# Two gated layers on one core: decays laid out by chunk, whole-chunk GpSimd operations, and a new order of all queues

## The chip, the core and the metric

The kernel runs on one core of a Trainium2 chip. The metric is the device time of one execution in microseconds, taken over several runs. A core has five instruction queues that run side by side and meet through semaphores: PE (TensorE, matrix products and transposes), VectorE (DVE in the profile), ScalarE (ACT), GpSimd (POOL) and SyncE (SP, which here issues all large transfers).

## The reference

Inputs are `x`, `r_gate` and `i_gate`, each 4 x 6336 x 256 float32, a vector `a_param` of 256, and the weights `w_val` (256 x 256), `conv_w` (5 x 256) and `w_out` (256 x 256). The first layer is a recurrence in time, the second a gated unit whose gate is a causal convolution of five taps:

```
log_a = 8 * sigmoid(r_gate) * log(clip(sigmoid(a_param)))
a = exp(log_a)
u = sqrt(max(1 - a*a, 1e-6)) * sigmoid(i_gate) * x
h[t] = a[t]*h[t-1] + u[t]                 # y = all h, for each batch
gate = sigmoid(sum over k of conv_w[k] * y[t-4+k])
out  = (gate * (y @ w_val)) @ w_out
```

## The kernel before

The four sequences are laid end to end: 25344 time steps of 256 channels. They are cut into 51 windows, mostly of 512 steps, and these into 28 chunks: chunks 0 and 1 of 256 steps, 2 of 512, 3 to 25 of two windows (1024 steps, chunk 26 has 512, chunk 27 256). Channels come in two halves of 128, called h. A window is loaded with time on the partitions; the recurrence wants channels on the partitions, so PE transposes in between.

One long string, `ORDER`, sets everything: it is a list of steps such as `ta.6` (a step's name, its chunk or window, sometimes the half) with the PSUM banks behind an `@`. The steps are written out in this order, so it is the order of each engine's queue. The steps of one chunk or window, with the lines of the profile:

- SP: `lr`, `li`, `lx` load a window of r, i and x (L292) into rings of four windows; `st` stores a window of the output (L546).
- ScalarE: `ta` and `tb` take tanh of r and i (L310, L313); `ex` makes the decays a with one exponential per half, for one chunk or a group of two (L378); `rt` takes the square roots of 1 - a*a for a batch of chunks (L405), usually three; `tg` is the gate's tanh (L502); `ca` copies an output window out of PSUM (L535). Tanh and exponential need one table of functions, the square root another, so there is a table load (L562) ahead of each run of `rt` and one behind it. `sa` squares a half of a chunk (L394, twice in the program).
- GpSimd: `sq` squares the decays of one half of one chunk into `ering` (L386); `pp` adds one to the tanh of i of a window (L320); `up` multiplies that by x (L332). `s_wcast` casts the weights once (L275 to L278).
- PE: `tr` transposes tanh of r (L357); `nt` transposes the square roots (L420), `xt` the gated inputs back (L461); `cv` is the convolution (L495), `vl` and `ou` the two products (L510, L525); `xp` carries x of three early windows through PSUM (L337). `wm` issues five products of 512 columns on the identity whose result nobody reads (L364).
- VectorE: `xg` multiplies the input by the root (L450); `sc` is the recurrence as a scan, one per half (L483); `gv` multiplies gate and value (L515); `cd` copies an output window (L533), where `ca` does not; `uv` is `up` for the three early windows (L346).

So a chunk goes: `lr`, `ta`, `tr`, `ex`, `sq`, `rt`, `nt`, `xg`, `xt`, `sc`, and then per window `cv`, `tg`, `vl`, `gv`, `ou`, `cd` or `ca`, `st`. The decays stand in `aring`, one half behind the other: `aring[:, h, ...]` has 5120 columns for each half, and a chunk has the same place in both. The squares of a chunk stand in `ering` with both halves side by side, so that one square root covers several chunks:

```
at = H * e_at[c] + h * clen[c]
return ering[:, at:at + clen[c]], aring[:, h, a_at[c]:a_at[c] + clen[c]]
```

## Time and profile before

| | |
|---|---|
| runs | 289.22, 287.34, 287.65 us; median 287.65 |
| profiled execution | span 286.4 us from the first to the last instruction; the page gives no other time for it |
| busy | PE 251.8 us, VectorE 246.8, ScalarE 273.6, GpSimd 241.6 |
| granted TensorE clock | 0.999 |
| transfers | 104.76 MB, mean 366 GB/s |

In the profile's rows a line such as "L378 ACT ACTIVATE aring<-banks,khf" is one group of instructions: the line of the kernel, the engine, the operation, what it writes and reads. A row of a timeline begins with the start in microseconds from the first instruction and the time that the row's instructions take together, and ends with the idle time of the engine ahead of it and what ended that. In a row of waits stand the total in microseconds, the number of waits and the longest. In a row of stretches each engine has its busy time in that stretch.

### The profile page before, as it was taken

The numbers are of one execution on the slowest core, as the hardware profiler recorded it, in microseconds if no ns is written. First come the engines' busy times: TensorE is split into PE (matmuls) and PEld (weight loads), VectorE is DVE, ScalarE is ACT, GpSimd is POOL, SyncE is SP. The second block draws the span as 40 slices with busy tenths as digits, with TensorE's granted clock in tenths as the row PEclk, the third lists the DMA queues.
The fourth block names the chain that finished last, engine by engine and source line by source line (L and its number), as shares of the span: only waits on it lengthen the run. The fifth ranks groups of instructions, "written<-read, shape, count | busy, mean of one in ns | idle before, by whom it ended". The sixth has DMA issues, their size and how long they took to land.

```text
span 286.4 us, 6382 instructions
## 1 busy us (share of the span) xinstructions
PE 251.8 (88%) x2552; PEld 171.1 (60%) x2576; DVE 246.8 (86%) x214; ACT 273.6 (96%) x198; POOL 241.6 (84%) x161
## 2 busy tenths in 40 slices
PE   1387778899999999988988999989989899999993
PEld 1253447456656767455756676656646774767562
DVE  4002898969999899999999999999999999999991
ACT  5999999999999999999999999999999999898984
POOL 1659589899999999999999999999996999874600
PEclk9999999999999999999999999999999999999999
DMA  7999999999999999999999999999999999994536
GB/s 243 384 373 407 409 403 408 388 366 376 410 408 366 418 367 392 414 410 334 405 364 413 411 332 356 420 416 419 415 401 333 359 416 406 364 356 170 192 150 256
DMA packets 29996, 104.76 MB, mean 366 GB/s; under 512 B 3335, under 2 KB 3854, under 8 KB 29966
## 3 DMA queue, kind: packets, MB, share of 16 engines
q1 hardware_dynamic: 29952, 104.35, 94.5%
q8 instruction: 20, 0.33, 0.5%
q14 instruction: 10, 0.08, 0.1%
q10 hardware_dynamic: 14, 0.01, 0.0%
HBM read 78.39 MB, written 25.95 MB: 364 GB/s over the span
## 4 chain that ended last, share of the span: by engine, by line
ACT 33%; PE 29%; DVE 14%; issue 12%; DMA 8%; SPq 1%; ACTq 0%; DVEq 0%
ACT ering L405 8%; PE banks L495 8%; DVE yring L483 7%; PE banks L525 7%; DMA rring<-in_r_gate_dram 6%; ACT tgring L502 6%; ACT taring L310 5%; ACT tbring L313 5%; ACT aring L378 5%; PE banks L510 5%; PE banks L461 3%; DVE tgring L515 3%; PE banks L420 3%; ACT L562 3%; DVE oring L533 2%
## 5 line engine op out<-in xcount | busy, mean ns | idle before, releaser
L386 POOL TENSOR_TENSOR ering<-aring 128x1024 f32<-128x1024 f32 (+2 forms) x54 | 91.5, 1714 | 16.7 <-ACT aring L378 16.4
L332 POOL TENSOR_TENSOR uring<-tbring,xring 128x1024 bf16<-128x1024 bf16 (+1 forms) x48 | 101.1, 2119 | 3.6 <-DMA xring<-in_x_dram 3.1
L483 DVE TENSOR_TENSOR_SCAN yring<-aring,yring,banks 128x1024 bf16<-128x1024 f32 (+5 forms) x50 | 101.7, 2064 | 2.1 <-PE banks L461 1.9
L495 PE MATMUL banks<-yring,diag 64*64 64x512 bf16 (+7 forms) x1080 | 62.1, 361 | 2.3 <-ACT aring L378 1.6
L515 DVE SCALAR_TENSOR_TENSOR tgring<-tgring,banks 128x1024 bf16<-128x1024 bf16 (+1 forms) x51 | 59.1, 1178 | 4.0 <-PE banks L510 3.4
L320 POOL TENSOR_SCALAR tbring<-tbring 128x1024 bf16<-128x1024 bf16 (+1 forms) x48 | 49.1, 1032 | 6.8 <-ACT tbring L313 6.7
L378 ACT ACTIVATE aring<-banks,khf 128x2048 f32<-128x2048 bf16 (+3 forms) x38 | 54.2, 1476 | 0.4 <-PE banks L357 0.3
L525 PE MATMUL banks<-wo,tgring 128*128 128x256 bf16 x396 | 51.0, 274 | 3.7 <-DVE tgring L515 3.2
L502 ACT ACTIVATE tgring<-banks 128x1024 bf16<-128x1024 f32 (+1 forms) x51 | 50.2, 1011 | 2.0 <-PE banks L495 1.9
L510 PE MATMUL banks<-yring,wv 128*128 128x512 bf16 (+4 forms) x192 | 48.1, 359 | 3.7 <-ACT tgring L502 1.9
L310 ACT ACTIVATE taring<-rring 128x2048 bf16<-128x2048 f32 (+2 forms) x28 | 47.9, 1718 | 1.4 <-DMA rring<-in_r_gate_dram 1.4
L525 PEld LDWEIGHTS <-tgring 128*128 128x128 bf16 x396 | 41.2, 114 | 13.1 <-DVE tgring L515 8.8
L313 ACT ACTIVATE tbring<-iring 128x2048 bf16<-128x2048 f32 (+2 forms) x28 | 48.2, 1726 | 0.0
L405 ACT ACTIVATE ering<-ering 128x4096 bf16<-128x4096 f32 (+5 forms) x16 | 44.8, 2840 | 0.1
L495 PEld LDWEIGHTS <-diag 64*64 64x64 bf16 x1080 | 29.0, 106 | 25.6 <-issue 9.9
L533 DVE COPY oring<-banks 128x1024 f32<-128x1024 f32 (+1 forms) x36 | 41.9, 1182 | 1.4 <-PE banks L525 0.7
L357 PE MATMUL banks<-ident_b,taring 128*128 128x128 bf16 x396 | 29.9, 230 | 9.4 <-ACT taring L310 6.7
L357 PEld LDWEIGHTS <-taring 128*128 128x128 bf16 x396 | 26.5, 103 | 14.2 <-ACT taring L310 7.4
L510 PEld LDWEIGHTS <-wv 128*128 128x128 bf16 x216 | 19.7, 98 | 24.5 <-issue 10.3
L450 DVE TENSOR_TENSOR uring<-banks,uring 128x2048 bf16<-128x2048 bf16 (+2 forms) x26 | 29.4, 1134 | 3.5 <-PE banks L420 3.2
L420 PE MATMUL banks<-ident,ering 128*128 128x128 f32 x192 | 28.3, 289 | 1.1 <-ACT ering L405 0.9
L461 PE MATMUL banks<-ident,uring 128*128 128x128 f32 x192 | 25.9, 276 | 3.5 <-DVE uring L450 2.8
(49 smaller groups left out, 154.0 us busy)
## 6 DMA issues: line engine op xcount, KB each, us to landing
rring<-in_r_gate_dram SPq DMA_DIRECT2D x48, 512.0 KB, 8.2
iring<-in_i_gate_dram SPq DMA_DIRECT2D x48, 512.0 KB, 8.7
xring<-in_x_dram SPq DMA_DIRECT2D x48, 512.0 KB, 8.2
out_dram<-oring SPq DMA_DIRECT2D x48, 512.0 KB, 6.5
rring<-in_r_gate_dram SPq DMA_DIRECT2D x3, 256.0 KB, 4.1
iring<-in_i_gate_dram SPq DMA_DIRECT2D x3, 256.0 KB, 6.5
xring<-in_x_dram SPq DMA_DIRECT2D x3, 256.0 KB, 8.5
out_dram<-oring SPq DMA_DIRECT2D x3, 256.0 KB, 5.2
```

What stands on the lines that cost most here:

```text
L310: nc.scalar.activation(**tangent(c, taring, NTR, rring, NRI))
L313: nc.scalar.activation(**tangent(c, tbring, NTI, iring, NII))
L332: nc.gpsimd.tensor_tensor(out=u, in0=t1, in1=xt, op=ALU.mult)
L378: nc.scalar.activation(out=dst, in_=src, func=ACT.Exp, scale=khf[:, h:h + 1], bias=khf[:, h:h + 1])
L386: nc.gpsimd.tensor_tensor(out=e, in0=a, in1=a, op=ALU.mult)
L405: nc.scalar.activation(out=ering[:].bitcast(BF16)[:, 4 * o:4 * o + 2 * n], in_=ering[:, 2 * o:2 * o + 2 * n], func=ACT.Sqrt, scale=-0.25, ...
L483: nc.vector.tensor_tensor_scan(out=yring[:, h, col:col + o1 - o0], data0=aring[:, h, a_at[c] + o0:a_at[c] + o1], data1=xT[:, o0:o1], initi ...
L495: nc.tensor.matmul(out=gp[oh * 64:oh * 64 + 64, h, a:b], lhsT=diag[half * 64:half * 64 + 64, h, k, :], rhs=yring[half * 64:half * 64 + 64, ...
L502: nc.scalar.activation(out=tgring[:, w % NTG, :, 0:wins[w]], in_=live.pop(("gp", w))[:, :, 0:wins[w]], func=ACT.Tanh, scale=0.5)
L510: nc.tensor.matmul(out=val[:, m, a:b], lhsT=wv[:, hk, m * P:(m + 1) * P], rhs=yring[:, hk, col:col + b - a], start=(hk == 0), stop=(hk == ...
L515: nc.vector.scalar_tensor_tensor(out=tgring[:, w % NTG, :, 0:wins[w]], in0=tgring[:, w % NTG, :, 0:wins[w]], scalar=1.0, in1=live.pop(("va ...
L525: nc.tensor.matmul(out=ops[:, j * D:(j + 1) * D], lhsT=gv[:, hk, j:wins[w]:J], rhs=wo[:, hk, :], start=(hk == 0), stop=(hk == H - 1))
```

## The change

The decays get the layout that the squares have: `aring` is one row of `H * NA` columns, and a chunk's two halves stand side by side. Then the decays of a whole chunk are one run of columns, and so are their squares: `sq.c` without a half squares both halves in one instruction (`sq.c.h` still exists for the small chunks). The new step `pc` adds one to the tanh of i for both windows of a chunk in one instruction. The steps `wm`, `sa` and the never used `sv` are gone. `s_kt` and `s_diag` name their banks. `ORDER` is written anew from end to end; it has 22 `pc` and 4 `pp` for 48 `pp`, 33 `sq` for 54, and 18 `ca` and 33 `cd` for 15 and 36.

```diff
-        aring = rings.tile([P, H, NA], FP32, name="aring")
+        aring = rings.tile([P, H * NA], FP32, name="aring")
...
+        def op_pc(c):
+            w, k = cwins[c][0], len(cwins[c])
+            t = tbring[:, place(w, NTI):place(w, NTI) + k, 0:wins[w] // P, :].rearrange("p w j d -> p (w j d)")
+            nc.gpsimd.tensor_scalar(out=t, in0=t, scalar1=1.0, scalar2=1.0, op0=ALU.mult, op1=ALU.add)
...
-        def op_wm(k, at):
-            for _ in range(5):
-                nc.tensor.matmul(out=banks[:, at], lhsT=ident_b[:], rhs=ident_b[:].unsqueeze(1).to_broadcast([P, 4, P]),
-                                 start=True, stop=True)
-
...
-            if len(at) == 1 or at[1] == at[0] + n:
-                dst = aring[:, h, at[0]:at[0] + n * len(at)].rearrange("c (k q j) -> c k q j", j=J, k=len(at))
-            else:
...
+            dst = aring[:, H * at[0]:H * (at[0] + n * len(at))].rearrange("c (k h q j) -> c k h q j", h=H, j=J, k=len(at))
+            dst = dst[:, :, h]
             nc.scalar.activation(out=dst, in_=src, func=ACT.Exp, scale=khf[:, h:h + 1], bias=khf[:, h:h + 1])
+
+        def decays(c, h):
+            at = H * a_at[c] + h * clen[c]
+            return aring[:, at:at + clen[c]]
 
         def squares(c, h):
             at = H * e_at[c] + h * clen[c]
-            return ering[:, at:at + clen[c]], aring[:, h, a_at[c]:a_at[c] + clen[c]]
-
-        def op_sq(c, h):
-            e, a = squares(c, h)
+            return ering[:, at:at + clen[c]], decays(c, h)
+
+        def both_squares(c):
+            n = clen[c]
+            return ering[:, H * e_at[c]:H * (e_at[c] + n)], aring[:, H * a_at[c]:H * (a_at[c] + n)]
+
+        def op_sq(c, *h):
+            e, a = squares(c, h[0]) if h else both_squares(c)
             nc.gpsimd.tensor_tensor(out=e, in0=a, in1=a, op=ALU.mult)
-
-        def op_sv(c, h):
...
-        def op_sa(c, h):
-            e, a = squares(c, h)
-            nc.scalar.activation(out=e, in_=a, func=ACT.Square)
...
-                                             data0=aring[:, h, a_at[c] + o0:a_at[c] + o1],
+                                             data0=decays(c, h)[:, o0:o1],
```

What the new order does to the queues is told at three places. The first is ScalarE near the start, from the tanh of the first large chunks on. Before, the square roots of batches 0 to 3 (chunks 0 to 4; 128x4096 is batch 3) stand in one run:

```order
L310 ACTIVATE taring<-rring 128x2048 x2
L313 ACTIVATE tbring<-iring 128x512
L313 ACTIVATE tbring<-iring 128x1024
L378 ACTIVATE aring<-banks,khf 128x2048 x2
L313 ACTIVATE tbring<-iring 128x2048
L310 ACTIVATE taring<-rring 128x2048 x2
L562 ACT_TABLE_LOAD
L405 ACTIVATE ering<-ering 128x512
L405 ACTIVATE ering<-ering 128x1024
L405 ACTIVATE ering<-ering 128x512
L405 ACTIVATE ering<-ering 128x4096
L562 ACT_TABLE_LOAD
```

Now the roots of the three small chunks come right behind the tanh of chunk 4, between two table loads of their own:

```order
L307 ACTIVATE tbring<-iring 128x512
L304 ACTIVATE taring<-rring 128x2048
L554 ACT_TABLE_LOAD
L397 ACTIVATE ering<-ering 128x512 x2
L397 ACTIVATE ering<-ering 128x1024
L554 ACT_TABLE_LOAD
L304 ACTIVATE taring<-rring 128x2048
L307 ACTIVATE tbring<-iring 128x2048
L307 ACTIVATE tbring<-iring 128x1024
L370 ACTIVATE aring<-banks,khf 128x2x1024 x2
```

and batch 3 has another pair of loads further on:

```order
L494 ACTIVATE tgring<-banks 128x1024
L370 ACTIVATE aring<-banks,khf 128x2x1024
L554 ACT_TABLE_LOAD
L397 ACTIVATE ering<-ering 128x4096
L554 ACT_TABLE_LOAD
L370 ACTIVATE aring<-banks,khf 128x2x1024
```

The roots of chunks 0 to 2 moved ahead of the two exponentials of chunks 3 and 4 (128x2048, now 128x2x1024) and of the tanhs around them, and the program has one pair of table loads more.

The second is GpSimd in the same part of the program. Before, the squares of chunks 3 and 4 (128x1024, one half each) stand among the additions (128x1024, one window each) and the products with x:

```order
L332 TENSOR_TENSOR uring<-tbring,xring 128x2x256
L386 TENSOR_TENSOR ering<-aring 128x1024 x2
L320 TENSOR_SCALAR tbring<-tbring 128x1024
L386 TENSOR_TENSOR ering<-aring 128x1024 x2
L320 TENSOR_SCALAR tbring<-tbring 128x1024
L332 TENSOR_TENSOR uring<-tbring,xring 128x2x2x256 x2
L386 TENSOR_TENSOR ering<-aring 128x1024
L320 TENSOR_SCALAR tbring<-tbring 128x1024
L275 CAST wv<-oring 128x2x128
L276 CAST wv<-oring 128x2x64
L277 CAST wv<-oring 128x2x64
L278 TENSOR_SCALAR wo<-oring 128x512
```

Now one addition and one square cover a chunk, and the casts of the weights stand between the squares of chunk 4 and chunk 3:

```order
L331 TENSOR_TENSOR uring<-tbring,xring 128x2x256
L320 TENSOR_SCALAR tbring<-tbring 128x2048
L386 TENSOR_TENSOR ering<-aring 128x2048
L269 CAST wv<-oring 128x2x128
L270 CAST wv<-oring 128x2x64
L271 CAST wv<-oring 128x2x64
L272 TENSOR_SCALAR wo<-oring 128x512
L386 TENSOR_TENSOR ering<-aring 128x2048
L314 TENSOR_SCALAR tbring<-tbring 128x1024
L331 TENSOR_TENSOR uring<-tbring,xring 128x2x2x256 x3
L386 TENSOR_TENSOR ering<-aring 128x2048 x2
```

The first large square moved behind the first large addition, and each covers what two instructions covered.

The third is ScalarE in the next chunks, from the roots of batch 4 on (2048 and 4096 columns). Before:

```order
L562 ACT_TABLE_LOAD
L405 ACTIVATE ering<-ering 128x2048
L405 ACTIVATE ering<-ering 128x4096
L562 ACT_TABLE_LOAD
L502 ACTIVATE tgring<-banks 128x1024
L313 ACTIVATE tbring<-iring 128x2048
L310 ACTIVATE taring<-rring 128x2048 x2
L502 ACTIVATE tgring<-banks 128x1024
L313 ACTIVATE tbring<-iring 128x2048
L378 ACTIVATE aring<-banks,khf 128x2048 x2
```

Now:

```order
L554 ACT_TABLE_LOAD
L397 ACTIVATE ering<-ering 128x2048
L397 ACTIVATE ering<-ering 128x4096
L554 ACT_TABLE_LOAD
L494 ACTIVATE tgring<-banks 128x1024 x2
L304 ACTIVATE taring<-rring 128x2048
L307 ACTIVATE tbring<-iring 128x2048
L527 COPY oring<-banks 128x1024
L307 ACTIVATE tbring<-iring 128x2048
L370 ACTIVATE aring<-banks,khf 128x2x1024 x2
```

A copy of an output window (window 6) moved onto ScalarE, between two tanhs; it was one of VectorE's.

More of the change, by code (lines that the diff above doesn't have):

```diff
@@ L99 @@
[L99 to L102 removed]
+s_ident s_small s_kt@0 s_diag@2 lr.0 lr.1 lr.2 li.1 lx.1 li.0 ta.0 ta.1 tr.1.1@7 lr.5 tr.0.1@6 tr.0.0@1 ta.2 tb.1 lr.6
+tr.1.0@3 ex.0.0 ex.1.0 tr.2.1@0 tr.2.0@2 ex.0.1 ex.2.1 ex.1.1 lx.0 li.3 lr.4 lr.3 s_wl.2 ex.2.0 tb.0 sq.1.0 sq.0.0
@@ new lines @@
+up.33 xg.18 li.38 lx.38 lr.43 lr.44 tb.19 ex.21.1 li.39 li.40 pc.19 ou.29.0@0,1 tr.21.0@2 sc.17.1 up.35 up.36
+xt.18@7,4 tr.22.1@5 sc.18.0 ex.21.0 ex.22.0 ca.29.0 tb.20 cv.32@0,1 tg.32 nt.19@2,3 ex.22.1 vl.30@0,1 sc.18.1 sq.21
+st.26 st.25 st.28 lx.37 st.23 ta.23 cv.31@6,7 tg.31 li.41 lx.39 li.42 lr.45 xg.19 xt.19@5,4 gv.30 sc.19.0 sq.22
+ou.30.0@2,3 tb.21 vl.31@6,7 vl.32@0,1 lr.46 sc.19.1 pc.20 gv.32 rt.9 cv.33@4,5 tg.33 gv.31 ou.32.0@0,1 cd.30.0
+cv.34@6,7 up.38 up.37 cd.32.0 ou.31.0@2,3 tg.34 cd.31.0 pc.21 lx.42 lx.40 nt.20@0,1 xg.20 vl.33@2,3 gv.33 lx.41 lr.47
@@ L103 @@
+gv.49 ou.49.0@0,1 ca.48.0 st.48 vl.50@4,5 tg.50 gv.50 ou.50.0@4 ca.49.0 st.49 ca.50.0 st.50
 """
@@ L229, in s_ident, with s_kt @@
             nc.gpsimd.tensor_copy(out=ident_b[:], in_=ident[:])
-        def s_kt():
-            kps = banks[:, 0]
+        def s_kt(at):
+            kps = banks[:, at]
             nc.tensor.transpose(out=kps[:, 0:H], in_=ap2[0:H, :], identity=ident[0:H, 0:H])
@@ L249, in s_kt, with s_diag @@
                                     scalar2=4.0 * math.log(1.0 - 1e-6), op0=ALU.max, op1=ALU.min)
-        def s_diag():
-            wps = banks[:, 1]
+        def s_diag(at):
+            wps = banks[:, at]
             for h in range(H):
```

131 lines of the change are left out of this document (57 added, 74 removed).

## The prediction

> **What bounds the kernel now.** I read the busy shares first, then the busy time by stretch, then what ScalarE waits for, and last the order of events at the start and behind the last large square root.
>
> ```profile
> PE 251.8 (88%) x2552; PEld 171.1 (60%) x2576; DVE 246.8 (86%) x214; ACT 273.6 (96%) x198; POOL 241.6 (84%) x161
> 160.00:180.00 20.00, 19.61 (x243) 13.50 (x238) 20.00 (x14) 19.98 (x15) 19.85 (x13) 1.00 0.97 362
> 240.00:260.00 20.00, 19.56 (x183) 13.45 (x185) 19.68 (x16) 17.56 (x16) 15.53 (x10) 1.00 0.98 359
> 260.00:284.00 24.00, 21.78 (x235) 14.58 (x235) 19.52 (x18) 20.77 (x23) 6.51 (x6) 1.00 0.49 189
> ```
>
> ScalarE is the busiest, 273.6 of 286.4 us. In the stretch 160 to 180 four engines are full at once (PE 19.61, VectorE 20.00, ScalarE 19.98, GpSimd 19.85 of 20), so the shares don't say which of them sets the pace. From 240 on ScalarE and GpSimd have holes and PE hardly any: 19.56 of 20, then 21.78 of the 22.8 up to its last product.
>
> ```profile
> 237.57 1.28 ACT L562 ACT_TABLE_LOAD   x1
> 238.87 5.33 ACT L405 ACTIVATE ering<-ering 128x6144 bf16<-128x6144 f32 x1
> 244.21 1.28 ACT L562 ACT_TABLE_LOAD   x1
> 243.04 1.07 PE L525 MATMUL banks<-wo,tgring 128*128 128x256 bf16 x8
> 244.25 1.23 PE L420 MATMUL banks<-ident,ering 128*128 128x128 f32 x8
> 282.17 0.61 PE L525 MATMUL banks<-wo,tgring 128*128 128x256 bf16 x4 [0.84 <-DVE tgring L515]
> 282.82 0.58 ACT L535 COPY oring<-banks 128x512 f32<-128x512 f32 x1 [0.88 <-PE banks L525]
> ```
>
> This is the hinge. The square root of batch 10 (chunks 23 to 25) ends at 244.20. PE finished an earlier output product at 244.1 and takes up the transposes of that result (L420) at once, then runs almost without a hole until 282.8; ScalarE's last copy ends at 283.4 and the last store follows to 286.4. So the span is the end of this square root plus 42.2 us, and those 42.2 us are PE's own work, 38.5 us, and the way out.
>
> ```profile
> ACT oring L535 <- PE banks L525: 2.8, 4, 1.1
> ACT tgring L502 <- PE banks L495: 1.9, 3, 1.1
> ACT ktmp L237 <- DVE ktmp L236: 1.9, 1, 1.9
> ACT taring L310 <- DMA rring<-in_r_gate_dram: 1.4, 4, 0.5
> ACT aring L378 <- PE banks L357: 0.3, 1, 0.3
> ```
>
> Before the hinge ScalarE waits only in the first 25 us; these rows are all its waits but the 0.7 us of the launch, and those for L535 and L502 lie behind it. The hinge's place is therefore the sum of what stands ahead of it on ScalarE, plus its waits at the start. Other engines have no hole there either, but what they must deliver is there in time: ScalarE waits for none of it.
>
> **The change part by part.** ScalarE's list of instructions ahead of the hinge: the first three chunks' square roots now run apart from batch 3's, which gives one more pair of table loads (20 behind the first one, where 18 stood); 17 large output copies where 14 stood, and the three more lie ahead of the hinge; and two squares (L394) move to GpSimd, one of 1024 columns ahead of the hinge, one of 256 behind it. All else is the same in number and size.
>
> ```profile
> L562 ACT ACT_TABLE_LOAD x18 | 23.1, 1283 | 0.3
> L535 ACT COPY oring<-banks 128x1024 f32<-128x1024 f32 x14 | 13.9, 1016 | 2.1 <-PE banks L525 2.0
> 253.02 1.92 ACT L535 COPY oring<-banks 128x1024 f32<-128x1024 f32 x2
> 229.97 1.12 ACT L394 ACTIVATE ering<-aring 128x1024 f32<-128x1024 f32 x1
> 230.92 1.98 ACT L313 ACTIVATE tbring<-iring 128x2048 bf16<-128x2048 f32 x1
> ```
>
> Two loads at 1.283 us and no overlap (237.57 to 238.87) are +2.6. A copy's mean is 1.016, but two in a row take 1.92 as neighbours overlap; three cost 2.7 to 3.0, I take +2.8. The square of 1.12 blocks ScalarE from 229.97 to 230.92: -1.0. Sum +4.4, bounds +4.2 and +4.7; nothing hides it, as ScalarE has no hole ahead of the hinge. The decays' new addresses alter neither the number of columns nor the order in which L378 reads them: 0.
>
> The Trainium skill ("ScalarE: Activation LUTs", section "What ACT_TABLE_LOAD costs") puts a switch of tables at about 1283 ns for the load and 1380 ns for a drain, 2.66 us together. The load agrees to the nanosecond, the drain isn't seen: the square root starts 0.02 us behind the end of its load, and all 18 loads together had 0.3 us of idle time ahead of them. By the page the two would cost 5.3 and not 2.6, and the forecast would be 296.0; I go by the row.
>
> GpSimd: whole chunks in one instruction.
>
> ```profile
> L386 POOL TENSOR_TENSOR ering<-aring 128x1024 f32<-128x1024 f32 x45 | 84.4, 1896 | 6.1 <-ACT aring L378 5.8
> L386 POOL TENSOR_TENSOR ering<-aring 128x512 f32<-128x512 f32 x4 | 4.2, 1039 | 2.9 <-ACT aring L378 2.9
> L320 POOL TENSOR_SCALAR tbring<-tbring 128x1024 bf16<-128x1024 bf16 x46 | 47.8, 1050 | 6.8 <-ACT tbring L313 6.7
> L320 POOL TENSOR_SCALAR tbring<-tbring 128x512 bf16<-128x512 bf16 x2 | 1.2, 619 | 0.0
> L533 DVE COPY oring<-banks 128x1024 f32<-128x1024 f32 x34 | 40.6, 1212 | 1.4 <-PE banks L525 0.7 <-issue 0.4
> L364 PE MATMUL banks<-ident_b 128*128 128x512 bf16 x85 | 21.1, 389 | 1.1 <-ACT aring L378 0.7 <-DVE yring L483 0.3
> ```
>
> The trace has no 2048 columns. From 512 to 1024 the square grows by 0.857 and the addition by 0.431; carried on, 3.61 and 1.91, each 0.18 to 0.19 less than two halves. Bounds: no saving at all, or 0.2 per pair. For 45 + 5 + 4 squares stand 23 + 6 + 4 (-0.8, with the two that came over), for 46 large additions 22 + 2 (-3.7): GpSimd does 4.5 us less, or at worst 2.5 more. VectorE loses three copies of 1.212 (-3.6). PE loses 85 filler products (-21.1). None of the three comes off the end: ScalarE sets the hinge, and the work placed behind it is the same on PE in both programs (3 transposes of norms, 5 of inputs, 9 gates, 11 values, 12 outputs, 4 transposes of r's tanh). The 0.41 us square taken from ScalarE there lies in PE's cover: 0.
>
> The price of a whole chunk: its square can't start on the first half. It waits for both exponentials.
>
> The start, where the order is new:
>
> ```profile
> 11.10 1.93 ACT L310 ACTIVATE taring<-rring 128x2048 bf16<-128x2048 f32 x1
> 13.40 1.91 ACT L310 ACTIVATE taring<-rring 128x2048 bf16<-128x2048 f32 x1 [0.38 <-DMA rring<-in_r_gate_dram]
> 24.55 1.91 ACT L310 ACTIVATE taring<-rring 128x2048 bf16<-128x2048 f32 x1 [0.28 <-DMA rring<-in_r_gate_dram]
> 27.77 5.61 ACT L405 ACTIVATE ering<-ering 128x512 bf16<-128x512 f32 x4
> 15.37 2.74 PE L357 MATMUL banks<-ident_b,taring 128*128 128x128 bf16 x24 [1.25 <-ACT taring L310]
> 27.69 1.06 PE L357 MATMUL banks<-ident_b,taring 128*128 128x128 bf16 x16
> 18.80 3.84 POOL L386 TENSOR_TENSOR ering<-aring 128x1024 f32<-128x1024 f32 x2 [0.31 <-ACT aring L378]
> 40.51 1.50 POOL L278 TENSOR_SCALAR wo<-oring 128x512 bf16<-128x512 f32 x1
> ```
>
> ScalarE's work up to the six small exponentials is the same set, so the next thing can start near 11.10 again: 0.6 (a small tanh) to 11.7, and the tanh of chunk 4, which needs loads 5 and 6 of r. Each goes into a slot that a tanh of chunks 1 and 2 frees (about 5.5 and 7 us), as before, where the later pair was there at 13.40; fewer bytes are ahead of it now, so I take 12.5: 0.8 to 0.9 us of waiting (bounds: 0, and 3.5 if the load took the median of 8.2 us that the loads' row further down has, from 7 on). Tanh 1.9, load 1.3, three small roots 2.3, load 1.3: 19.3. Three tanhs (1.9, 1.9, 1.1) to 24.1, an exponential of 2.05 to 26.1. The second exponential of chunks 3 and 4 needs 16 transposes on PE that stand behind the scans' inputs and two f32 products. Without the filler PE's transposes run as in 15.37, 24 in 2.74 us or 114 ns each, not 16 in 1.06: 1.8 us, ready at about 26.9. That is +0.8 (bounds 0, 2). Against these stand the waits that go: 0.38 ahead of 13.40 and 0.28 ahead of 24.55, -0.7. Net +1.0; bounds -1.7 (every wait of the rows for L310 and L378, 1.4 and 0.3, gone) and +4.8.
>
> The exponential so ends at 28.9. GpSimd then squares chunk 4 (3.6), casts weights (2.5, the last of them in the row of 40.51) and squares chunk 3 (3.6): 38.6, where the first of these squares stood at 18.80. ScalarE has eight things to do until then (two tanhs of r and one of i, three gates, an exponential, a load: 11.2), and asks at 40.1. So 1.5 us of cover remain; with it gone the root waits by what is missing. From there GpSimd has about 219 us of work left (237.1 less some 18 done) and ScalarE over 235 (277.7 less some 40), so GpSimd stays ahead.
>
> Middle: +0.3 for single waits of a new order (bounds 0, as there are none now, and 4). Tail 0 (bounds -1 and +2).
>
> 286.4 + 4.4 + 1.0 + 0.3 = 292.1 for the span. The page gives no time of its own for the profiled execution beside the span; the median of the runs is 287.65, 1.25 above it, and I carry that: 293.3 us, 2.0% slower. A measurement of this kernel can tell about 1% from no change.
>
> **The rivals.**
>
> *The end shrinks* (not slower). VectorE's scans begin with the first square root.
>
> ```profile
> 29.94 0.69 DVE L483 TENSOR_TENSOR_SCAN yring<-aring,banks 128x256 bf16<-128x256 f32 x1 [0.41 <-PE banks L461]
> ```
>
> That root would come at 15.7 instead of 27.8, so VectorE and PE start some ten microseconds sooner, and have 3.6 and 21.1 us less to do. If the hinge finds them with their work done, ScalarE's waits behind it go: of the 39.2 us from 244.2 to 283.4 the stretches' rows give ScalarE 34.1 us of work (their sum less the 4.2 ahead of the hinge), so 5.1 us are waits. 292.1 - 5.1 + 1.25 = 288.3. For it: VectorE is as full as ScalarE in the middle. Against it: PE was ready for the hinge already (243.04 + 1.07), and what is queued behind it on PE is the same 38.5 us of back-to-back work. It decides from the point where PE's stretch behind the root falls under 38.5.
>
> *ScalarE runs faster beside idler neighbours* (about the same). The tanh of 2048 columns takes 1.90 to 1.93 at the start and 1.98 at 230.92. If all its work came 1% nearer to the first figure, 2.7 us go: 290.6. Against it: the means of the forms lie near the start's values already.
>
> *Loads come late* (slower still).
>
> ```profile
> SPq L546 <- DVE oring L533: 39.2, 19, 5.4
> SPq L546 <- ACT oring L535: 28.8, 11, 8.0
> rring<-in_r_gate_dram SPq DMA_DIRECT2D x48, 512.0 KB, 8.2
> ```
>
> SP issues loads and stores in one order; a store that waits for its copy (39.2 and 28.8 us, the longest 5.4 and 8.0) holds every load behind it. Now it does so beside a copy on ScalarE that may stand behind a root of 5.3 us. A load of r is issued when the tanh two chunks ahead frees its slot and is needed two chunks later, about 17.6 us (219.7 us from 24.55 to 244.2 over 25 chunks, doubled); landing takes 8.2, so a hold of 9.4 us is free. Two in a row (8.0 + 5.4) make ScalarE wait 4.0: 297.3. For it: every queue is new; against it: ScalarE, the consumer, gets slower, and before no load was late past 25 us.
>
> **How the numbers follow.** Forecast 0.61 with a range of its own of 291 to 296; the end shrinks 0.08; faster ScalarE 0.10; late loads or holes of that size 0.21. The range takes in both sides' nearer cases: 289.5 to 298.0. More than 1% faster (under 284.8) needs the first rival and a smooth start together: 0.03. Within 1% (to 290.5): the rest of that rival, the second one, and the forecast's edge: 0.15. Slower by more: 0.82.
>
> **What would show it.** Right: ScalarE's busy time near 278, 21 table loads, the root of batch 10 ending at 249 to 251, and 41 to 43 us from there to the end; GpSimd busy near 237 and square mean 3.6; the second large exponential waiting under a microsecond, GpSimd done before the root asks. Wrong: the root of batch 10 ending under 247, or less than 40 us behind it; new rows of ScalarE's waits for loads or GpSimd in the middle that add up to over 2 us; or a 2048-column square far from 3.6.

## The result and the profile after

The changed kernel takes 298.14 us (median of four runs, 296.77 to 299.99) where the kernel before, run beside it, takes 287.68: a ratio of 1.0356 with an interval of 1.0296 to 1.0417. It is slower by 3.6%. The forecast was 293.3 us, so the direction holds and the size is 4.8 us short; 298.14 lies 0.14 above the upper end of the range, and by the ratio (1.0356 times 287.65 is 297.9) just inside it. The ratios of the experiments leave out two executions that ran slowly beside the others of their kernel, 299.56 us with the first load of before and 301.23 with the merge undone, and the medians count them.

The profiled execution of after has a span of 295.0 us and a time of 296.77. The busy shares, in the order of the row quoted from before:

```profile
span 295.0 us, 6147 instructions
PE 237.1 (80%) x2467; PEld 164.1 (56%) x2491; DVE 244.9 (83%) x211; ACT 277.9 (94%) x201; POOL 237.4 (80%) x118
```

ScalarE has 277.9 us where the prediction worked out 277.7 to 278, GpSimd 237.4 for 237.1. PE and VectorE lose less than the prediction took off them: PE 14.7 us (251.8 to 237.1) for 21.1, VectorE 1.9 (246.8 to 244.9) for 3.6. Every engine but ScalarE has less to do, and the span is 8.6 us longer. The hinge of the prediction, the end of the square root of batch 10, is where these 8.6 us have to be looked for:

```profile
247.21 5.34 ACT L397 ACTIVATE ering<-ering 128x6144 bf16<-128x6144 f32 x1
```

The root starts at 247.21 instead of 238.87 and ends at 252.55 instead of 244.20: 8.35 of the 8.6 us lie ahead of it. The prediction had named 249 to 251 as a sign of being right, and this end is 1.6 us past it. Cutting both programs there, and once more at 30 us, gives the whole account. The columns are the stretch, its length, busy time of PE, weight loads, VectorE, ScalarE and GpSimd, the clock, and the transfers. First before, then after:

```profile
0.00:30.00 30.00, 16.04 (x101) 10.21 (x102) 5.78 (x25) 25.70 (x26) 18.19 (x22) 1.00 0.95 355
30.00:244.20 214.20, 198.50 (x2076) 135.37 (x2093) 205.88 (x162) 213.77 (x136) 205.56 (x128) 1.00 1.01 391
244.20:286.40 42.20, 37.30 (x377) 25.55 (x382) 35.11 (x29) 34.13 (x37) 17.84 (x13) 0.99 0.66 245
```

```profile
0.00:30.00 30.00, 12.40 (x106) 8.11 (x110) 11.45 (x33) 23.63 (x26) 9.30 (x17) 1.00 0.87 322
30.00:252.55 222.55, 187.47 (x1993) 130.02 (x2002) 198.35 (x152) 220.10 (x141) 208.19 (x89) 0.99 0.98 379
252.55:295.00 42.45, 37.20 (x377) 25.93 (x382) 35.06 (x29) 34.14 (x36) 19.93 (x14) 0.99 0.65 252
```

Ahead of the hinge ScalarE works 25.70 + 213.77 = 239.47 us before and 23.63 + 220.10 = 243.73 after: +4.26. Its idle time there is 4.30 + 0.43 = 4.73 before and 6.37 + 2.45 = 8.82 after: +4.09. Behind the hinge ScalarE has the same 34.1 us of work and PE the same 37.2, and the stretch is 42.45 for 42.20. So the span grows by work (4.3), waits (4.1) and nearly nothing at the end (0.25). The waits have names (total, number, longest):

```profile
ACT taring L304 <- DMA rring<-in_r_gate_dram: 5.8, 4, 2.9
ACT oring L527 <- PE banks L517: 2.8, 5, 0.9
ACT tgring L494 <- PE banks L487: 1.6, 2, 1.3
ACT tbring L307 <- DMA iring<-in_i_gate_dram: 0.7, 1, 0.7
ACT aring L370 <- PE banks L356: 0.7, 2, 0.4
```

The first row had 1.4 us before. Four waits for loads of r cost 5.8 us now; most of the rows for L494 and L527 lies behind the hinge, as before. Behind the first 3 us ScalarE waits for neither GpSimd nor VectorE.

### The profile page after: what moved, and what is told of

It reads as the page before. It is cut to its first block, busy times and chain, and to the rows that moved or that the text cites. A ratio compares the mean times of both kernels' runs of the same rounds, so it can differ in the third digit from the quotient of the medians.

```text
span 295.0 us, 6147 instructions
## 1 busy us (share of the span) xinstructions
PE 237.1 (80%) x2467; PEld 164.1 (56%) x2491; DVE 244.9 (83%) x211; ACT 277.9 (94%) x201; POOL 237.4 (80%) x118
## 4 chain that ended last, share of the span: by engine, by line
ACT 28%; PE 20%; DMA 19%; DVE 15%; issue 10%; POOL 6%; SPq 1%; ACTq 0%; DVEq 0%; POOLq 0%
DMA iring<-in_i_gate_dram 10%; ACT tbring L307 7%; DMA rring<-in_r_gate_dram 6%; DVE tgring L507 6%; PE banks L517 5%; PE banks L487 5%; ACT aring L370 5%; ACT taring L304 5%; ACT tgring L494 4%; DVE oring L525 4%; DVE yring L475 4%; PE banks L502 4%; POOL uring L331 4%; ACT L554 3%; DMA out_dram<-oring 3%
## 5 line engine op out<-in xcount | busy, mean ns | idle before, releaser
L386 POOL TENSOR_TENSOR ering<-aring 128x2048 f32<-128x2048 f32 (+2 forms) x33 | 90.3, 2747 | 14.1 <-ACT aring L370 13.8
L487 PE MATMUL banks<-yring,diag 64*64 64x512 bf16 (+7 forms) x1080 | 62.8, 362 | 9.8 <-DVE yring L475 3.8
L502 PE MATMUL banks<-yring,wv 128*128 128x512 bf16 (+4 forms) x192 | 49.4, 362 | 11.1 <-ACT tgring L494 4.9
L320 POOL TENSOR_SCALAR tbring<-tbring 128x2048 bf16<-128x2048 bf16 x22 | 41.8, 1900 | 17.1 <-ACT tbring L307 15.9
L494 ACT ACTIVATE tgring<-banks 128x1024 bf16<-128x1024 f32 (+1 forms) x51 | 50.2, 1008 | 1.9 <-PE banks L487 1.6
L487 PEld LDWEIGHTS <-diag 64*64 64x64 bf16 x1080 | 30.7, 106 | 32.7 <-issue 17.8
L525 DVE COPY oring<-banks 128x1024 f32<-128x1024 f32 (+1 forms) x33 | 38.4, 1185 | 5.0 <-PE banks L517 4.4
L412 PE MATMUL banks<-ident,ering 128*128 128x128 f32 x192 | 29.2, 295 | 11.0 <-ACT ering L397 8.8
L356 PE MATMUL banks<-ident_b,taring 128*128 128x128 bf16 x396 | 28.7, 226 | 8.0 <-ACT taring L304 5.6
L412 PEld LDWEIGHTS banks<-ident,ering 128*128 128x128 f32 x192 | 25.2, 209 | 17.3 <-ACT ering L397 11.7
L356 PEld LDWEIGHTS <-taring 128*128 128x128 bf16 x396 | 25.5, 101 | 13.4 <-ACT taring L304 6.7
```

The source lines that it names most:

```text
L386: nc.gpsimd.tensor_tensor(out=e, in0=a, in1=a, op=ALU.mult)
L412: nc.tensor.transpose(out=bank[:, k:k + P], in_=ering[:, e + q:e + wins[w] // 2:nq], identity=ident[:])
L487: nc.tensor.matmul(out=gp[oh * 64:oh * 64 + 64, h, a:b], lhsT=diag[half * 64:half * 64 + 64, h, k, :], rhs=yring[half * 64:half * 64 + 64, ...
L494: nc.scalar.activation(out=tgring[:, w % NTG, :, 0:wins[w]], in_=live.pop(("gp", w))[:, :, 0:wins[w]], func=ACT.Tanh, scale=0.5)
L502: nc.tensor.matmul(out=val[:, m, a:b], lhsT=wv[:, hk, m * P:(m + 1) * P], rhs=yring[:, hk, col:col + b - a], start=(hk == 0), stop=(hk == ...
```

## The experiments

Kernels named below as built on before keep its order of steps but for what the edit shows; those built on after likewise. Ratios are to the kernel before in the same series, and a difference to it in microseconds is the ratio times 287.7.

### The merge alone, in the old order

The layout, whole-chunk squares and whole-chunk additions, each at the place of the last of the steps that it replaces; nothing else of the order is touched.

```diff
-... ex.3.1 sq.3.0 wm.5@6 lx.3 wm.3@6 tb.3 sq.3.1 wm.9@6 wm.6@6 ta.6 pp.4 sq.4.1 ta.5 ...
+... ex.3.1 wm.5@6 lx.3 wm.3@6 tb.3 sq.3 wm.9@6 wm.6@6 ta.6 pc.3 ta.5 ...
```

> The layout by chunk and the merged GpSimd operations (22 additions and 22 squares that cover a whole chunk) alone, put into the queue order of before; fillers and the two squares on ScalarE stay. Theory (ScalarE's list sets the end, the merge lies off it): 287.7 us within 1, GpSimd's busy time about 7 us lower (43 pairs at 0.18), no new wait of ScalarE. Rival 1 (whole-chunk squares come late for the roots): ScalarE waits for GpSimd ahead of roots, 2 to 4 us in sum, 290 to 292. Rival 2 (GpSimd sets the pace before): 283 to 285.

295.02 us, ratio 1.0252 [1.0216, 1.0289]. GpSimd's busy time fell to 235.0 as it should, and the kernel is 7.2 us slower: the first rival's direction, by more than it said and not in its way: the roots wait 0.6 us for GpSimd, where it had 2 to 4. There is no new list on ScalarE and no new order in it; these 7.2 us come from parts of the change that the prediction priced at nothing. ScalarE has waits that before lacks or has shorter (the first row was 1.9 us there):

```profile
ACT tgring L510 <- PE banks L503: 3.4, 6, 1.1
ACT tbring L310 <- POOL uring L334: 1.4, 1, 1.4
ACT aring L378 <- DVE yring L491: 1.4, 1, 1.4
ACT ering L413 <- POOL ering L394: 0.6, 1, 0.6
```

Its waits for loads of r rise as well, from 1.4 to 3.3 us, and those for transposes from 0.3 to 1.6. The third row is the odd one: an exponential (L378) that waits for a scan.

### Three copies on ScalarE

Before, with the copies of three output windows moved from VectorE to ScalarE.

```diff
-... cd.10.0 ... cd.15.0 ... cd.24.0 ...
+... ca.10.0 ... ca.15.0 ... ca.24.0 ...
```

> The kernel before with three output copies (windows 10, 15 and 24) moved from VectorE to ScalarE at their places. Theory (ScalarE's list sets the place of the root of batch 10): that root ends 2.7 to 3.0 us later than 244.2, time 290.5 (+2.8). Rival (VectorE or GpSimd set the pace as much, and VectorE has 3.6 us less to do): 287 to 288, no change.

290.06 us, 1.0067 [1.0045, 1.0088]: +1.9. The span grew by as much, and from the first large roots to the root of batch 10 ScalarE needs 2.5 us more. Work added to ScalarE comes off the end for the most part, 1.9 us of the 2.8 expected; VectorE's 3.4 us less (243.4) bring nothing.

### One more pair of table loads

Before, with a pair of loads (the exponential's set, the root's set) behind the root of batch 7.

```diff
-... rt.7 ca.19.0 ...
+... rt.7 tl ca.19.0 ...
```

> The kernel before with one more pair of table loads, back to back behind the root of batch 7. Theory: the root of batch 10 ends 2.6 us later, time 290.3 (+2.6). By the Trainium skill's price of a switch of tables (ScalarE: Activation LUTs, What ACT_TABLE_LOAD costs: 2.66 us each) +5.3, 293.0. Rival (other engines catch up, the end shrinks): 288 or less.

291.40 us, 1.0106 [1.0076, 1.0137]: +3.0, and +3.8 on the span of the profiled execution. Between the roots of batches 7 and 8 ScalarE needs 4.1 us more. Its busy time rises by 2.7 (276.3), the two loads; the rest are 1.3 us of waits:

```profile
ACT aring L378 <- PE banks L357: 1.3, 2, 0.7
```

So a pair costs its own 2.6 us and, at this place, a wait behind it for PE's transposes. The loads delay a copy on ScalarE (L535) that frees PSUM banks; PE stands idle for it from 153.05 to 155.69, and from 156.7 on its granted clock is half for some 3.4 us.

The drain that the Trainium skill gives ("ScalarE: Activation LUTs", section "What ACT_TABLE_LOAD costs": 1380 ns beside a load of 1283 ns) makes 5.3 for the pair, an estimate from the page's two figures; no such idle time stands at these loads, here or in after, whose 20 loads have 0.4 us ahead of them in all:

```profile
L554 ACT ACT_TABLE_LOAD x20 | 25.7, 1283 | 0.4
```

### The merge, with five instructions less on ScalarE

The first experiment's kernel, with the two squares of ScalarE on GpSimd and three copies on VectorE.

```diff
-... ca.19.0 ... ca.23.0 ... ca.33.0 ... sa.25.1 ... sq.25.0 ... sa.27.1 ...
+... cd.19.0 ... cd.23.0 ... cd.33.0 ... sq.25 ... sq.27.1 ...
```

> As m1_merge_old_order, and ScalarE loses work: its two squares go to GpSimd, which the merge has made idler, and the three output copies ahead of the root of batch 10 (windows 19, 23, 33) go to VectorE. Theory: ScalarE has 3.8 us less ahead of that root (1.0 + 2.8), time 283.9. Rival (VectorE, full from 160 to 240, takes over as bound with 3.6 us more): 286 to 289.

300.34 us, 1.0429 [1.0390, 1.0468]: its median is 5.3 us above that of the merge alone. My theory fails here, and the rival's 286 to 289 as well. ScalarE's list is shorter and the kernel longer:

```profile
PE 257.1 (86%) x2576; PEld 173.0 (58%) x2576; DVE 250.8 (84%) x217; ACT 271.1 (90%) x193; POOL 237.2 (79%) x118
```

```profile
ACT aring L378 <- PE banks L359: 7.6, 5, 3.0
ACT aring L378 <- DVE yring L491: 2.7, 2, 1.4
```

ScalarE is down to 271.1 us and waits 7.6 us for transposes, and VectorE has 250.8 us now. The longest of these waits can be followed:

```profile
156.26 2.33 DVE L541 COPY oring<-banks 128x1024 f32<-128x1024 f32 x2
157.61 1.77 PE L428 MATMUL banks<-ident,ering 128*128 128x128 f32 x8 [2.19 <-DVE oring L541]
162.22 2.06 ACT L378 ACTIVATE aring<-banks,khf 128x2048 f32<-128x2048 bf16 x1 [3.04 <-PE banks L359]
```

A copy that ScalarE made right behind the root (at 155.59 in the merge alone) is now the first of the two in the first row and stands behind a scan (154.01 to 156.35). PE waits 2.19 us for it, where it waited 0.58 for ScalarE's, and its granted clock is then 0.50 from 158 to 160 and 0.65 from 160 to 162. The exponential gets its transposes 3.04 us late. What stands behind the other waits was not followed; that the pace is set by whichever of the full engines is handed more work is my reading of the whole.

### After, with three copies back on VectorE

```diff
-... ca.6.0 ... ca.18.0 ... ca.21.0 ...
+... cd.6.0 ... cd.18.0 ... cd.21.0 ...
```

> The changed kernel with three output copies (windows 6, 18 and 21) given back to VectorE at their places. Theory: 2.8 us less on ScalarE ahead of the root of batch 10, so it ends near 249.8 instead of 252.55; time 2.8 us under the changed kernel's (its profiled execution 296.8, median 298.1). Rival (the order's late loads and VectorE set the pace): within 1 us of it.

296.18 us, 1.0289 [1.0271, 1.0308]. The ratio is 1.9 us below after's, but their intervals overlap, and the span (294.8) and the root of batch 10 (246.94 for 247.21) hardly move. The work that left ScalarE came back as waits:

```profile
ACT aring L372 <- PE banks L358: 2.3, 4, 0.9
ACT aring L372 <- DVE yring L477: 2.2, 2, 1.2
ACT tgring L496 <- PE banks L489: 2.2, 4, 1.3
```

The second row is a wait for scans that after does not have. By the profiled execution (296.59 for 296.77) the rival is right; by the ratios the gain lies between the rival's 1 us and the theory's 2.8 and cannot be told from either. In the profiled execution the copies' 2.8 us do not come back.

### After, with the first load of before

Window 2 of r, the largest of the first three, is loaded first, as in before.

```diff
-... s_diag@2 lr.0 lr.1 lr.2 li.1 ...
+... s_diag@2 lr.2 lr.0 lr.1 li.1 ...
```

> The changed kernel with the load of r of window 2 moved to the first place of all loads, as before the change. Theory (the tanh of chunk 2 waits 2.89 us because its load is third and shares the transfers with three more): that wait shrinks to under 0.6, the loads of windows 5 and 6 are issued earlier, and everything behind is 1.5 to 2.2 us earlier: 1.5 to 2.2 us under the changed kernel. Rival (the bytes ahead of chunk 4's tanh set the start anyway): the wait goes over to chunk 4's tanh, under 0.5 us gained.

297.50 us (294.56 to 299.56), 1.0307 [1.0264, 1.0351]: 1.4 us below after by the ratios, with intervals that overlap. In the profiled execution (296.97) the 2.9 us wait for that load is gone and the first roots start at 15.35 instead of 17.24, but batch 3 starts at 39.55 for 40.14, batch 4 at 63.25 for 63.18, batch 10 at 247.42 for 247.21. The time won at the start is lost a few instructions later:

```profile
26.95 2.06 ACT L372 ACTIVATE aring<-banks,khf 128x2048 f32<-128x2048 bf16 x1 [1.58 <-PE banks L358]
```

The second exponential now waits 1.58 for the transposes. The load made the wait at the start; the hinge of this execution does not move with it.

### After, with filler products near the start

```diff
+... wm.0@5 wm.1@5 wm.2@5 ... wm.3@2 ... wm.4@0 wm.5@0 ...
```

> The changed kernel with 30 filler products on PE put back near the start (behind the first transposes, behind the convolution of window 2 and behind the product of window 1). Theory: the changed kernel's slower executions (299 to 300 with a granted clock of 0.975, beside 296.8 with 0.993) come from PE's idle stretches after the start; with the filler the clock is 0.99 or more in every run, the root of batch 10 stays at 252.5 within 0.5, and all times lie near 296.8. Rival (the clock has nothing to do with the filler): clocks and times scatter as without it.

297.65 us, 1.0344 [1.0324, 1.0365]; span 295.2, root of batch 10 at 247.47, granted clock 0.980 to 0.988 in its five runs. The 30 products neither shorten this span nor bring the clock back to the 0.999 of before, so the theory fails. The five clocks lie between the two groups of after (0.975 and 0.993). Where the products stand they do what I had hoped: the granted clock from 35 to 45 us is 1.00, where after has 0.84 and 0.82, and it falls at 70 and 81 us instead. What it does there is told in the last section.

### The layout alone, and each half of the merge alone

All in the old order. The first has nothing but the new addresses: the same 976 steps, the same sizes.

```diff
-        aring = rings.tile([P, H, NA], FP32, name="aring")
+        aring = rings.tile([P, H * NA], FP32, name="aring")
...
-                dst = aring[:, h, at[0]:at[0] + n * len(at)].rearrange("c (k q j) -> c k q j", j=J, k=len(at))
+            dst = aring[:, H * at[0]:H * (at[0] + n * len(at))].rearrange("c (k h q j) -> c k h q j", h=H, j=J, k=len(at))
+            dst = dst[:, :, h]
...
-            return ering[:, at:at + clen[c]], aring[:, h, a_at[c]:a_at[c] + clen[c]]
+            return ering[:, at:at + clen[c]], decays(c, h)
```

> The layout by chunk alone in the queue order of before; every GpSimd operation keeps its size. Theory A (the 7 us that the merge cost in the old order come from GpSimd's longer steps): 287.7 within 0.7. Theory B (they come from the layout, because an exponential now waits for more scans before it may overwrite decays): 291 to 295, with ScalarE's waits for the scan (L483's successor) in it.

293.91 us, 1.0206 [1.0186, 1.0226]: the layout by itself costs 5.9 us in the old order, with the same instructions and, within 0.1 us, the same busy times of ScalarE, VectorE and GpSimd. The roots say where. Up to batch 6 they run 0.84 us ahead of before; batch 7 starts 1.26 behind it (148.28 for 147.02), batches 8 and 9 stay there, batch 10 is 3.92 behind (242.79 for 238.87) and the span 5.5. So three short places make the loss, 2.1, 2.6 and 1.6 us. The first, before:

```profile
132.40 2.33 DVE L483 TENSOR_TENSOR_SCAN yring<-aring,yring,banks 128x1024 bf16<-128x1024 f32 x1
133.56 2.07 ACT L378 ACTIVATE aring<-banks,khf 128x2048 f32<-128x2048 bf16 x1
```

and with the new layout, ScalarE, VectorE and GpSimd:

```profile
131.56 2.34 DVE L494 TENSOR_TENSOR_SCAN yring<-aring,yring,banks 128x1024 bf16<-128x1024 f32 x1
133.99 2.06 ACT L381 ACTIVATE aring<-banks,khf 128x2048 f32<-128x2048 bf16 x1 [1.25 <-DVE yring L494]
140.79 7.45 POOL L397 TENSOR_TENSOR ering<-aring 128x1024 f32<-128x1024 f32 x4 [2.44 <-ACT aring L381]
148.28 5.33 ACT L416 ACTIVATE ering<-ering 128x6144 bf16<-128x6144 f32 x1 [0.84 <-POOL ering L397]
```

Before, the exponential starts at 133.56 while a scan runs until 134.73. Here it waits 1.25 us for that scan (to 133.90) and GpSimd, which ran without a hole there in before, waits 2.44 us for the exponential of the other half (138.65 to 140.71) before its first square (`sq.15.1`), so the root waits 0.84 more: 2.09 us in all, and 1.26 + 0.84 is 2.10. The step order tells what the two have to do with each other: the exponential (`ex.15.1`) writes one half of chunks 15 and 16, over old decays of chunks 10 and 11, and the scan (`sc.11.0`) reads the other half of chunk 11. In the old layout these were ranges apart. In the new one an exponential of one half of two chunks writes two pieces with a gap, and the gap is the other half. The trace fits waits that count the range from the first to the last column written. I tested that reading by no kernel of its own, but two more waits of GpSimd in the same trace bear it out:

```profile
224.27 1.89 POOL L386 TENSOR_TENSOR ering<-aring 128x1024 f32<-128x1024 f32 x1
228.41 4.27 ACT L381 ACTIVATE aring<-banks,khf 128x2048 f32<-128x2048 bf16 x3
230.56 1.89 POOL L397 TENSOR_TENSOR ering<-aring 128x1024 f32<-128x1024 f32 x1 [5.08 <-ACT aring L381]
179.23 3.75 POOL L397 TENSOR_TENSOR ering<-aring 128x1024 f32<-128x1024 f32 x2 [1.77 <-ACT aring L381]
```

The first row is before: `sq.23.1` starts as soon as its own half is there (the exponential from 222.11 to 224.20). With the new layout it waits 5.08 us, until the exponential of half 0 of chunks 23 and 24 has ended (the first of the three at 228.41), and its own columns lie in that exponential's gap. The last row is `sq.20.0`, in the gap of `ex.19.1` (177.08 to 179.14): it starts behind that exponential's end, while in before it started at 176.27 in the middle of it (175.86 to 177.97).

So GpSimd falls behind: at 209 it is 3 us behind before, ScalarE only 1.26, and at 234.5 it is 6.3. VectorE waits for its products twice:

```profile
216.50 1.22 DVE L461 TENSOR_TENSOR uring<-banks,uring 128x2048 bf16<-128x2048 bf16 x1 [1.72 <-POOL uring L337]
234.61 1.23 DVE L461 TENSOR_TENSOR uring<-banks,uring 128x2048 bf16<-128x2048 bf16 x1 [1.74 <-POOL uring L337]
```

What VectorE delivers late goes through PE's convolution to the gate's tanh, which waits 1.15 us at 220.13 and 1.09 at 240.46; that is most of the second step of 2.64 us. The third, behind the hinge, is two longer waits for PE: 1.71 us ahead of a copy at 254.89, where before has 1.09, and 1.21 ahead of the gate's tanh at 257.11, where it has 0.23.

The squares of whole chunks on top of the layout:

```diff
-... sq.3.0 ... sq.3.1 ... sq.4.1 ... sq.4.0 ...
+... sq.3 ... sq.4 ...
```

> Layout by chunk and whole-chunk squares in the old order; the additions stay one per window. Theory A, with the squares as its cause (a square that waits for both exponentials holds GpSimd's queue 2 to 3 us, three to five times): 291 to 295. If the additions are the cause: within 1 of m8_layout_only.

296.57 us, 1.0289 [1.0261, 1.0318], 2.4 us above the layout alone. GpSimd has 3.3 us less to do (238.4) and VectorE waits longer for it:

```profile
220.25 1.23 DVE L459 TENSOR_TENSOR uring<-banks,uring 128x2048 bf16<-128x2048 bf16 x1 [2.99 <-POOL uring L335]
221.53 1.79 PE L470 MATMUL banks<-ident,uring 128*128 128x128 f32 x8 [2.64 <-DVE uring L459]
225.51 1.02 ACT L511 ACTIVATE tgring<-banks 128x1024 bf16<-128x1024 f32 x1 [3.35 <-PE banks L504]
```

One product of GpSimd that comes 2.99 us late for VectorE makes PE idle 2.64 and the gate's tanh wait 3.35. My reading, from the sizes alone: a square of 3.6 us that stands ahead of a product holds it twice as long as one of 1.9. Each also stands at the place of the later of the two that it replaces, and the run does not tell the one from the other. GpSimd's waits for exponentials are not longer in sum (24.5 us for the layout's 24.9).

The additions of whole chunks on top of the layout:

```diff
-... pp.4 ... pp.3 ... pp.7 ... pp.8 ...
+... pc.3 ... pc.5 ...
```

> Layout by chunk and whole-chunk additions in the old order; the squares stay one per half. If the squares are the cause: within 1 of m8_layout_only, or 1 under it as GpSimd has 4 us less to do. If the additions are (they pull the second window's addition ahead of a product and so delay x's slots and the loads): 290 to 295.

293.54 us, 1.0197 [1.0176, 1.0218]: 0.3 us below the layout alone, no difference that can be told. Layout, squares and additions add to 5.9 + 2.4 - 0.3 = 8.0 us, and the merge as a whole had 7.2.

### After, with a shorter list on ScalarE

Three copies (windows 6, 18, 21) are left out, so these outputs are not written, and batch 5's roots are computed as exponentials, which needs no table of its own.

```diff
-... ca.6.0 ... ca.18.0 ... ca.21.0 ...
+... cn.6.0 ... cn.18.0 ... cn.21.0 ...        # the copy is not issued
-                                     func=ACT.Sqrt, scale=-0.25, bias=0.25)
+                                     func=ACT.Exp if b == 5 else ACT.Sqrt, scale=-0.25, bias=0.25)
```

> The changed kernel without what its ScalarE list has more: the output copies of windows 6, 18 and 21 are left out, and batch 5's roots are computed as exponentials, which saves a pair of table loads; the times alone count. Theory (ScalarE's list ahead of the root of batch 10 sets the end): 5.4 us less there, that root ends near 247.2, time 291.4 to 292.7. Rival (the new order's waits on the other engines fill up what is taken off, as when the copies went to VectorE): less than 2 us gained, 295 to 297.

294.44 us (293.06 to 296.30), 1.0236 [1.0204, 1.0267]: 3.5 us below after by the ratios, between theory and rival. ScalarE is left with 273.9 us, 4.0 less than in after and as much as before had, and the kernel is still 2.4% slower than before. The profiled execution was its slowest, 296.30; in it the root of batch 10 starts at 246.76, only 0.45 ahead of after's, and waits have taken most of what the list gave up. They add to 16.2 us, 3.1 more than in after; the gate's tanh waits 2.7 us for 1.6, the exponentials 2.7 for 0.7:

```profile
ACT tgring L496 <- PE banks L489: 2.7, 3, 1.3
ACT aring L372 <- PE banks L358: 2.7, 5, 1.6
```

### After, with the merge undone in place

The layout and the new order stay; each whole-chunk square and addition is issued as two halves at the same place.

```diff
-... pc.3 ... sq.4 s_wcast sq.3 ...
+... pp.3 pp.4 ... sq.4.0 sq.4.1 s_wcast sq.3.0 sq.3.1 ...
```

> The changed kernel with the merge undone in place: each whole-chunk square is two squares of a half, each whole-chunk addition two of a window, at the same places of the new order; the layout stays. Theory (in the new order GpSimd is off the path): GpSimd's busy time about 8 us higher, time within 1 us of the changed kernel's 296.8 to 298.1. Rival 1 (the merge costs here too, through steps that wait longer): 293 to 295. Rival 2 (the merge pays here): 300 or more.

298.20 us, 1.0360 [1.0319, 1.0400], and after itself 1.0356. GpSimd has 6.6 us more (244.0), the root of batch 10 starts at 247.18 for 247.21. In the new order the merge makes no difference that can be told; the two intervals together would hide some 2 us.

No kernel of these beats the one before.

## Why the prediction was right in direction and short by 4.8 us

**Right: the list on ScalarE.** Forecast +4.4 ahead of the hinge, measured +4.26. Two table loads are two loads (20 behind the first one, 1283 ns each), without a drain. Three copies and a pair of loads added to before cost 1.9 and 3.0 us by themselves, so additions to ScalarE do reach the end, in the old order at least.

**Right: the end.** 42.45 us behind the hinge, forecast 42.2 with a tail of 0. The rival that the end shrinks is out: PE's work there is 37.20 us for 37.30.

**Right: GpSimd's sizes, and that they bring nothing.** Carried on from 512 and 1024 columns, the square of 2048 was to take 3.61 and the addition 1.91:

```profile
L386 POOL TENSOR_TENSOR ering<-aring 128x2048 f32<-128x2048 f32 x23 | 82.6, 3601 | 5.0 <-ACT aring L370 4.7
L320 POOL TENSOR_SCALAR tbring<-tbring 128x2048 bf16<-128x2048 bf16 x22 | 41.8, 1900 | 17.1 <-ACT tbring L307 15.9 <-DMA xring<-in_x_dram 1.2
```

They take 3.60 and 1.90, and the 4.2 us that GpSimd saves show nowhere. Batch 3's root was to be asked for at 40.1 with GpSimd done by then; it starts at 40.14 without a wait. That the time agrees so well is luck: the second exponential ended at 29.60 instead of 28.9, and the eight things behind it took 10.5 us instead of 11.2. GpSimd was done at 39.12, not 38.6. The rival that ScalarE runs faster beside idler neighbours is out too: the tanh of 2048 columns has a mean of 1917 ns for r and 1922 for i, and had 1918 and 1927.

**Mis-sized: the start, +1.0 forecast, +2.1 measured.** Of the forecast, +0.8 stands for transposes that were to run slowly without the filler products. They did not:

```profile
26.44 1.06 PE L356 MATMUL banks<-ident_b,taring 128*128 128x128 bf16 x16
```

The sixteen that the second exponential needs take 1.06 us, as sixteen did with filler ahead of them, and the exponential waits 0.29. The step that failed is the first sentence of that part, that the work up to the six small exponentials is the same set and so ends near 11.10 again. The set is the same and its first load is not:

```profile
7.74 1.06 ACT L304 ACTIVATE taring<-rring 128x1024 bf16<-128x1024 f32 x1 [2.89 <-DMA rring<-in_r_gate_dram]
12.34 0.65 ACT L307 ACTIVATE tbring<-iring 128x512 bf16<-128x512 f32 x1
14.02 1.91 ACT L304 ACTIVATE taring<-rring 128x2048 bf16<-128x2048 f32 x1 [1.03 <-DMA rring<-in_r_gate_dram]
```

The load of window 2 went from the head of the queue to the third place, the tanh on it waits 2.89 us, and the work that was to end at 11.10 ends at 12.34. In all, ScalarE's waits for loads of r in the first 30 us rise from 1.38 to 4.49 us; against that, a wait for VectorE in the set-up, of which the forecast says nothing, falls from 1.85 to 0.81. I read ScalarE's order and passed over SP's.

**Mis-sized: the middle, +0.3 forecast, +2.0 measured.** Two loads that come late make it, one of r and one of i:

```profile
146.19 1.91 ACT L304 ACTIVATE taring<-rring 128x2048 bf16<-128x2048 f32 x1 [1.29 <-DMA rring<-in_r_gate_dram]
180.83 1.91 ACT L307 ACTIVATE tbring<-iring 128x2048 bf16<-128x2048 f32 x1 [0.71 <-DMA iring<-in_i_gate_dram]
```

1.29 and 0.71 are 2.0 us. This is the rival of the late loads, at half of the price that it had. Loads stand in one queue with the stores, and the stores still wait for their copies:

```profile
SPq L538 <- ACT oring L527: 34.8, 11, 8.3
```

34.8 us of waits for ScalarE's copies, where 28.8 were; the load and the store that made these two late were not traced one by one.

**Mis-sized: from the span to the time, +1.25 forecast.** All four runs of after lie 1.77 to 1.81 us above their spans, and the runs of before beside the experiments 1.75 to 1.99 above theirs; the 1.25 set a median against the span of another execution. And two of the four have a longer span, 297.6 and 298.2 at mean granted clocks of 0.975 and 0.976, beside 295.0 and 295.1 at 0.993 and 0.994. The median between them is 3.1 above the span that the sum was made for. That is 1.9 of the missing 4.8 us; the start gives 1.1, the middle 1.7, the end 0.25 and the list takes 0.1 back.

**Wrong: "The decays' new addresses alter neither the number of columns nor the order in which L378 reads them: 0."** Both halves of the sentence hold and the conclusion doesn't follow. Alone, in the old order, the addresses cost 5.9 us, more than any term of the sum, because they change who must wait for whom. In after itself no exponential waits for a scan and no root for a square, so this cost is not to be seen there as a wait; either it does not arise in the new order, or the order pays for it elsewhere. Whether the new order with the old layout would be faster was not run and stays open.

**Half wrong: "ScalarE sets the hinge."** It holds, for the most part, for the work that was added. For work that is taken off, three kernels say otherwise: three copies less bring 0.2 on the span of the profiled execution and 1.9 in the ratio, three copies and two loads less bring 3.5 in the ratio and 0.45 on the hinge of the profiled execution, and in the merged kernel in the old order 3.2 us less on ScalarE made it 5.3 slower. The additions were tried in the old order without the merge and the savings in other orders, so what part the order has in this is not separated. The prediction's stretch from 160 to 180 with four full engines had said as much.

## What to carry to other kernels

In these kernels with four full engines, work added to one of them came off the end for the most part, and work taken from it or moved to another only in part or not at all, so a sum of additions forecast better than a sum of savings. A copy that changes its engine also changes when its PSUM bank comes free; look for who waits for it. A new layout is priced by its waits before its elements: here an instruction that writes every second piece of a buffer touched, for those who wait, what lies between. And an order written anew is read on the queue that issues the transfers first; there the start and the middle went off course.

## What the runs showed of the hardware that was not expected

The clock granted to PE is halved for some 3.4 us at a time, and that near a hole in its work, not where it is busiest:

```profile
38.88 0.58 PE L502 MATMUL banks<-yring,wv 128*128 128x512 bf16 x1 [1.69 <-ACT aring L370]
40.53 1.66 PE L356 MATMUL banks<-ident_b,taring 128*128 128x128 bf16 x16
160.00:180.00 20.00, 18.36 (x217) 14.48 (x220) 17.94 (x17) 19.97 (x15) 16.26 (x7) 1.00 0.83 319
```

In after PE stands idle from 37.19 to 38.88. The clock is 0.59 from 38 to 40 and 0.55 from 40 to 42, and 1.00 on both sides, as it is where PE has 18.36 of 20 us of work. Sixteen transposes take 1.66 us in that stretch and 1.06 at 26.44. Such stretches begin in or shortly behind holes: of 2.64 us with the added pair of loads, of 2.23 in the merge alone (177.04 to 179.27; half clock from 179.9), of 2.19 in the merge with less on ScalarE, and of 2.13 and 2.19 with the filler (67.31 to 69.44 and 77.42 to 79.61). Not every hole brings one: in after a hole of 2.14 us at 68.85 passes at full clock, and before has one of 1.69 at 24.21 and a mean of 0.999. And in the merge with less on ScalarE one begins at 181.9 behind holes of only 1.22 and 0.72 us. What decides between them stays open.

Executions of after lie 3 us apart with mean clocks of 0.993 and 0.975. By these two means the longer ones have some 10 us more at half clock, about three more such stretches; that is an estimate, and where they lie is not known, as only a shorter one was profiled.

On GpSimd a fixed part of 0.18 to 0.19 us goes into each of these operations, and the rest grows with the columns up to 2048 as it does from 512 to 1024; so merging two saves that fixed part at most, and holds the engine twice as long at a time. Over a whole program the 22 merged squares saved 3.3 us of busy time here and the 22 merged additions 3.4, some 0.15 us each.
